# Tokens in runs of nine on a partition, and kv on 64x64 quarters

## The chip, the cores and the metric

The kernel runs on one core of one Trainium2 chip. The metric is device time in microseconds of a whole execution; the kernel before takes 289.03 us (median of 3 runs, 288.88 to 289.15). A profiled execution shows what each engine does: TensorE (PE, with its weight loads as PEld), VectorE (DVE), ScalarE (ACT), GpSimd (POOL) and the queues that issue transfers (SP, and ACT's own).

## What is computed

Attention in Shen's efficient form for 8 batches, 8 heads, 576 tokens and 64 dimensions: a softmax of q over the dimensions, a softmax of k over the tokens, a 64x64 matrix kv for each head, and x = q kv. Then a feed-forward block (FFN) with a gelu gate on the 4608 tokens of 512 features, with an inner width of 1536.

```python
q_s = np.exp(q - np.max(q, axis=-1, keepdims=True));  q_s /= np.sum(q_s, axis=-1, keepdims=True) + 1e-09
k_s = np.exp(k - np.max(k, axis=2, keepdims=True));   k_s /= np.sum(k_s, axis=2, keepdims=True) + 1e-09
kv = np.einsum('bhsd,bhse->bhde', k_s, v)
x  = np.einsum('bhsd,bhde->bhse', q_s, kv).transpose(0, 2, 1, 3).reshape(B * S, H * D)
g = x @ w_gate
out = 0.5 * g * (1.0 + erf(g / np.sqrt(2))) * (x @ w_val) @ w_out
```

Inputs and output are float32 in DRAM; the kernel multiplies in float16 and sums in float32.

## The kernel before

**Order.** The FFN runs over groups of 512 tokens: the first 512 tokens of each of eight batches, and one group (number 8, tile `xtr`) made of the 64 tokens that each batch leaves over. The groups come in the order 0 to 6, 8, 7. Groups 0 and 1 use plain products; from group 2 on, and partly in the output of group 1, products are by Strassen's scheme (7 products of half size, with sums of operands made on DVE, ACT and POOL). From group 2 on, the order of all work is written out in strings (`PROG`); in groups 0 and 1 attention for the next batch is hung into the FFN's loop by `plan`, filled with `at(...)` and played by `ride` (L1061 to L1108).

**Layout of q, k, v.** A batch's token number is m*9 + n, with m from 0 to 63. `load` (L180) puts each m on two partitions: an even one with token chunks n = 0 to 3 behind a padding, an odd one with n = 4 to 8. So there are five chunks of 128 partitions (`NC`), all eight heads lie on each partition, and one load is two transfers over 64 partitions, with runs of 1024 and 1280 bytes. The padding is written once by memsets (L151, L152, L158 and, for the second k buffer, on POOL): -1e30 for k, 0 for v and q. In batch 0, the odd half of each load goes by ACT's queue, the rest by SP's.

**Attention.** `exp` runs on ACT over the whole tile or half of the heads, padding included. For q, `norm_sum` and `norm_pair` (L241, L250) sum over the dimensions and take reciprocals on DVE, and `norm_mul` (L263) scales on POOL or DVE. `cast_v` copies v to float16, with a column of ones that gives the sum over k. kv is then made in one of three ways. Batch 0: `kv0_mm` (L340), ten 128x64 matmuls for each head pair, with k's sums from `ksum_mm` (L327). Batch 1: `kv_mm` (L304), five 128x128 matmuls with 130 columns for each head pair, of which a mask keeps the diagonal blocks. Batches 2 to 7: `unit_kv4` (L361), 40 matmuls with 128 partitions of k, 64 columns of weights and 65 columns of v into one PSUM bank, and `kv4_norm` (L374), one reciprocal and one product on DVE. q is transposed on TensorE in batches 0 and 1 (`unit_t`, L391) and by one transposing transfer in later ones (`unit_td`, L415).

x comes from `unit_x` (L438) in batches 0 and 1, one matmul with a block-diagonal 128x128 kv for each head pair, 512 columns. From batch 2 on `unit_x4` (L454) makes it with 64x64 quarters: eight narrow matmuls for the 64 remaining tokens (`psxr`) and eight of 512 columns (`psx`). A copy by ACT and DVE puts x into `xt`, in the order of tokens in which `store` (L585) writes the rows out again.

**The start.** L1001 to L1055: SP and ACT issue q, k, v; ACT loads its table for exp and writes the tile `warm`, on which TensorE runs 15 + 2 + 3 warm-up matmuls; weights follow on SP's queue, the first 256 columns of the gate's and the value's weights in two pieces by columns. `ffn_first0` (L551) then starts the FFN of batch 0 with the two upper head pairs' x still to be made between its matmuls, and `ffn_first` (L527) does the same in batch 1, whose list `first1` (L1077) has half of that batch's transposes, kv and x.

**Batch 0 to batch 1.** The output products of batch 0 (`psy`, L579) run in two sweeps over four blocks of 128 tokens; between them `plan` puts the first half of batch 1's attention, and `evac` (L988) takes the results out. POOL casts the last three pieces of the output weights. Sums of weights for Strassen's scheme (`sum_w`, `sum_wgv`) are spread over groups 0 and 1; the last two of `sum_wgv` (L642) run on DVE in the output of group 1.

Of the kernel before, what the change touches and what calls it, by code (L numbers as in the profile page):

```python
# [9 lines left out]
f32 = mybir.dt.float32  # L10
# [8 lines left out]
def kernel(  # L19
# [23 lines left out]
    NM = 4  # L43
    NC = NM + 1
    MAIN = NM * P
    REM = S - MAIN
    VW = D + 1
    WCH = [0, 128, 256] + list(range(512, F + 1, 256))
    NW = len(WCH) - 1
# [69 lines left out]
    mask = const.tile([P, 2, D], f32)  # L119
# [3 lines left out]
    for i in range(2):  # L123
        eq_b.append(const.tile([P, NC, C], f16, name=f"eq{i}"))
    ek_b.append(const.tile([P, NC, C], f16, name="ek"))
    v16_b.append(const.tile([P, NC, H, VW + 1], f16, name="v16"))
# [5 lines left out]
    eq0r = const.tile([P, C], f16)  # L132
    ld_b = {nm: [const.tile([P, H, NC * D], f32, name=f"{nm}t{i}") for i in range(n)]
# [5 lines left out]
    cc_b = [x.rearrange("p n c -> p (n c)").bitcast(f32)[:, 0:1024].rearrange(  # L139
# [5 lines left out]
    q0r = [x[0:64].rearrange("p (h d) -> p h d", d=D) for x in (  # L145
        kt1[:, 36 * P:].bitcast(f32), eq_b[1].rearrange("p n c -> p (n c)").bitcast(f32)[:, 1024:])]
# [4 lines left out]
    nc.vector.memset(ld_b["k"][0][:, :, 0:D], -1e30)  # L151
    nc.vector.memset(ld_b["v"][0][:, :, 0:D], 0.0)  # L152
    nc.vector.memset(tiny, 0.0)
    nc.vector.memset(ones, 1.0)
    nc.vector.memset(mask, 0.0)
    nc.vector.memset(mask[0:64, 0, :], 1.0)
    nc.vector.memset(mask[64:128, 1, :], 1.0)
    nc.vector.memset(ld_b["q"][0][:, :, 0:D], 0.0)  # L158
    make_identity(nc, ident)
    nc.gpsimd.memset(v16_b[0][:, :, :, D:D + 1], 1.0)  # L160
    nc.gpsimd.memset(ld_b["k"][1][:, :, 0:D], -1e30)
# [8 lines left out]
    QUAD = 2  # L170

    def heads(x, b, h0, h1):

        if b >= QUAD:
            return x.rearrange("p (t c) x -> p c t x", t=2)[:, h0 // 2:h1 // 2]
        return x[:, h0:h1]

    tiles = {}

    def load(src, nm, b, h0, h1, n0):  # L180
        tiles[(nm, b)] = buf(ld_b[nm], b)
        for t, c0 in ((0, n0), (1, 1)):
            (nc.scalar if b == 0 and t == 1 else nc.sync).dma_start(  # L183
                out=tiles[(nm, b)][t:P:2, h0:h1, c0 * D:NC * D],
                in_=src[b, h0:h1].rearrange("h (m n) d -> m h (n d)", n=NT)[
                    :, :, (4 * t + c0) * D:(4 * t + NC) * D])

# [6 lines left out]
    def load_w_gv(c):  # L194
        for w, nm in ((moe_w_gate, "wg"), (moe_w_val, "wv")):
            t = wst_tile(f"{nm}st", HP, WCH[c + 1] - WCH[c])
            nc.sync.dma_start(
                out=t, in_=w.rearrange("(ci p) f -> p ci f", p=P)[:, :, WCH[c]:WCH[c + 1]])
            wst[(nm, c)] = t
# [9 lines left out]
    def cast_w(nm, c, eng="pool"):  # L209
        dst = (wg_sb if nm == "wg" else wv_sb)[:, :, WCH[c]:WCH[c + 1]]  # L210
        copy_on(eng, dst, wst[(nm, c)])

    def load_w_o(c):
        t = wst_tile("wost", 2, C)
        nc.sync.dma_start(
            out=t, in_=moe_w_out.rearrange("(fi p) m -> p fi m", p=P)[:, 2 * c:2 * c + 2, :])
        wst[("wo", c)] = t

    def cast_w_o(c, eng="pool"):
        copy_on(eng, wo_sb[:, 2 * c:2 * c + 2, :], wst[("wo", c)])  # L220


    def exp(nm, b, h0=0, h1=H, n0=0):
        dst = ek_b[0] if nm == "k" else buf(eq_b, b)
        o, i = (("p n (c t d) -> p c t n d", "p c t (n d) -> p c t n d") if b >= QUAD else
                ("p n (h d) -> p h n d", "p h (n d) -> p h n d"))
        nc.scalar.activation(  # L227
            out=dst[:, n0:NC, h0 * D:h1 * D].rearrange(o, d=D, **({"t": 2} if b >= QUAD else {})),
            in_=heads(tiles[(nm, b)], b, h0, h1)[..., n0 * D:NC * D].rearrange(i, d=D),
            func=ACTF.Exp)  # L230

    def cast_v(b, h0, h1, eng="pool"):
        if h1 - h0 > 2 and (eng == "pool" or b >= QUAD):
            for h in range(h0, h1, 2):
                cast_v(b, h, h + 2, eng)
            return
        copy_on(eng, v16_b[0][:, :, h0:h1, 0:D].rearrange("p n h d -> p h n d"),
                (tiles[("v", b)][:, h0 // 2::4] if b >= QUAD else tiles[("v", b)][:, h0:h1]).rearrange(
                    "p h (n d) -> p h n d", d=D))

    def norm_sum(b, hp, n0=0):  # L241
        n = NC - n0
        e = buf(eq_b, b)[:, n0:NC, hp * P:(hp + 1) * P].rearrange("p n (h d) -> p n h d", d=D)
        rq = att.tile([P, n, 2], f32, name="rq", tag="rq", bufs=4)
        nc.vector.reduce_sum(rq, e, axis=mybir.AxisListType.X)
        rrq = att.tile([P, n, 2], f32, name="rrq", tag="rrq", bufs=4)
        nc.vector.reciprocal(out=rrq, in_=rq)
        st[(b, "norm", hp)] = (e, rrq, n)

    def norm_pair(b, g, n0, engs):  # L250

        n = NC - n0
        e = buf(eq_b, b)[:, n0:NC, 2 * g * P:(2 * g + 2) * P].rearrange("p n (h d) -> p n h d", d=D)
        rq = att.tile([P, n, 4], f32, name="rq2", tag="rq2", bufs=2)
        nc.vector.reduce_sum(rq, e, axis=mybir.AxisListType.X)  # L255
        rrq = att.tile([P, n, 4], f32, name="rrq2", tag="rrq2", bufs=2)
        nc.vector.reciprocal(out=rrq, in_=rq)
        for j in range(2):
            st[(b, "norm", 2 * g + j)] = (e[:, :, 2 * j:2 * j + 2], rrq[:, :, 2 * j:2 * j + 2], n)
        for j, eng in enumerate(engs):  # L260
            norm_mul(b, 2 * g + j, eng)

    def norm_mul(b, hp, eng="dve"):  # L263
        e, rrq, n = st[(b, "norm", hp)]
        (nc.gpsimd if eng == "pool" else nc.vector).tensor_tensor(  # L265
            out=e, in0=e, in1=rrq.unsqueeze(-1).to_broadcast((P, n, 2, D)), op=ALU.mult)

    def norm_mul2(b, hp, cut):
        e, rrq, n = st[(b, "norm", hp)]
        for eng, r in ((nc.vector, slice(0, cut)), (nc.gpsimd, slice(cut, n))):  # L270
            eng.tensor_tensor(out=e[:, r], in0=e[:, r], in1=rrq[:, r].unsqueeze(-1).to_broadcast(
                (P, r.stop - r.start, 2, D)), op=ALU.mult)

    def norm(b, hp, eng="dve", n0=0):
        norm_sum(b, hp, n0)
        norm_mul(b, hp, eng)

    def load_rem0():
        for h0 in (0, 4):
            nc.sync.dma_start(out=q0r[h0 // 4], in_=q[0, h0:h0 + 4].rearrange(  # L280
                "h (m n) d -> m h (n d)", n=NT)[:, :, 0:D])

    def exp_rem0():
        for i in range(2):
            nc.scalar.activation(
                out=eq0r[0:64, i * 4 * D:(i + 1) * 4 * D].rearrange("p (h d) -> p h d", d=D),
                in_=q0r[i], func=ACTF.Exp)

    def norm_rem0():
        e = eq0r[0:64].rearrange("p (h d) -> p h d", d=D)  # L290
        rq = att.tile([64, H], f32, name="rq0", tag="rq0", bufs=1)
        nc.vector.reduce_sum(rq, e, axis=mybir.AxisListType.X)
        rrq = att.tile([64, H], f32, name="rrq0", tag="rrq0", bufs=1)
        nc.vector.reciprocal(out=rrq, in_=rq)
        st["rrq0"] = rrq

    def norm_rem0_mul():
        e = eq0r[0:64].rearrange("p (h d) -> p h d", d=D)
        nc.gpsimd.tensor_tensor(
            out=e, in0=e, in1=st["rrq0"].unsqueeze(-1).to_broadcast((64, H, D)), op=ALU.mult)  # L300
# [3 lines left out]
    def kv_mm(b, g, j):  # L304
        if (b, "pskv", g) not in st:
            st[(b, "pskv", g)] = small([P, 2, 2 * VW], f32, "pskv")
        hp = 2 * g + j
        for n in range(NC):
            nc.tensor.matmul(
                st[(b, "pskv", g)][:, j, :], ek_b[0][:, n, hp * P:(hp + 1) * P],  # L310
                v16_b[0][:, n, 2 * hp:2 * hp + 2, 0:VW],
                start=(n == 0), stop=(n == NC - 1))

    def kv_norm(b, g):
        pskv = st[(b, "pskv", g)]
        rck = att.tile([P, 2], f32, name="rck", tag="rck")
        nc.vector.reciprocal(out=rck, in_=pskv[:, :, D])
        for j in range(2):
            kv_sb = att.tile([P, 2, D], f16, name="kv_sb", tag="kv", bufs=8)
            nc.vector.scalar_tensor_tensor(  # L320
                out=kv_sb,
                in0=pskv[:, j, :].rearrange("p (h e) -> p h e", e=VW)[:, :, 0:D],
                scalar=rck[:, j:j + 1], in1=mask, op0=ALU.mult, op1=ALU.mult)
            st[(b, "kv", 2 * g + j)] = kv_sb
# [849 lines left out]
```

## Time and profile before

| | |
|---|---|
| runs, median of 3 | 289.03 us (288.88 to 289.15) |
| span of the profiled execution | 286.9 us |
| outside of the span, median less span | 2.1 us |
| PE, DVE, ACT, POOL busy | 277.9, 248.3, 209.8, 137.9 us |
| DRAM read, written | 37.75 MB, 9.44 MB |

The span is the profiled execution's own time; what lies around it is start and end of the program. TensorE is the busiest engine. The profile's slices are 7.2 us each. Some stretches of it:

| stretch, us | what runs | PE busy | DVE busy | POOL busy | GB/s |
|---|---|---|---|---|---|
| 0 to 5 | loads, memsets, first warm-up matmul | 0.09 | 1.95 | 1.34 | 140 |
| 5 to 15 | attention of batch 0 | 9.90 | 7.07 | 4.36 | 363 to 389 |
| 15 to 18.6 | first FFN matmuls, rest of x of batch 0 | 3.60 | 1.84 | 2.37 | 389 |
| 18.6 to 36.9 | gate and value of batch 0 | 18.30 | 11.53 | 12.92 | 391 |
| 36.9 to 48.5 | output of batch 0, attention of batch 1 | 11.60 | 9.77 | 5.85 | 390 |
| 48.5 to 71 | gate and value of batch 1 | 22.50 | 17.64 | 20.36 | 325 |
| 71 to 82 | output of batch 1, kv and x of batch 2 | 10.85 | 10.80 | 3.36 | 77 |
| 82 to 287 | the rest | 201.07 | 187.69 | 87.34 | 127 |

A matmul's duration in the profile runs from its start to its modelled end, and neighbours overlap: what a step costs on TensorE is read from the start of its first matmul to the start of the next step's first.

### The profile page before, as it was taken

The numbers are of one execution on the slowest core, as the hardware profiler recorded it, in microseconds if no ns is written. First come the engines' busy times: TensorE is split into PE (matmuls) and PEld (weight loads), VectorE is DVE, ScalarE is ACT, GpSimd is POOL, SyncE is SP. The second block draws the span as 40 slices with busy tenths as digits, with TensorE's granted clock in tenths as the row PEclk, the third lists the DMA queues.
The fourth block names the chain that finished last, engine by engine and source line by source line (L and its number), as shares of the span: only waits on it lengthen the run. The fifth ranks groups of instructions, "written<-read, shape, count | busy, mean of one in ns | idle before, by whom it ended". The sixth has DMA issues, their size and how long they took to land.

```text
span 286.9 us, 6704 instructions
## 1 busy us (share of the span) xinstructions
PE 277.9 (97%) x2581; PEld 216.4 (75%) x2581; DVE 248.3 (87%) x497; ACT 209.8 (73%) x370; POOL 137.9 (48%) x128
## 2 busy tenths in 40 slices
PE   3999999999999999999999999999999999999994
PEld 1544445445888888888888888888888888888883
DVE  2854788877999999979989998999999799998993
ACT  3773367884798889978998899799794577716740
POOL 1557845987339721865864258542553104110110
PEclk9999999999999999999999999999999999999999
DMA  6999999999139916159149853690304030003303
GB/s 215 375 380 386 401 393 390 394 328 243 35 139 339 258 34 223 78 101 321 45 98 308 289 164 150 182 249 2 147 6 90 0 150 0 2 0 77 73 2 146
DMA packets 54623, 51.74 MB, mean 180 GB/s; under 512 B 18496, under 2 KB 50496, under 8 KB 54592
## 3 DMA queue, kind: packets, MB, share of 16 engines
q1 hardware_dynamic: 52864, 49.49, 54.0%
q10 hardware_dynamic: 1728, 1.84, 2.0%
q8 instruction: 20, 0.33, 0.5%
q14 instruction: 11, 0.09, 0.1%
HBM read 37.75 MB, written 9.44 MB: 164 GB/s over the span
## 4 chain that ended last, share of the span: by engine, by line
PE 91%; DVE 5%; ACT 1%; issue 1%; ACTq 1%; DVEq 0%
PE psa L670 24%; PE psc L670 12%; PE psA L749 12%; PE psg L511 7%; PE psv L511 7%; PE psC L749 6%; PE psb L670 6%; PE psy L579 4%; PE psB L749 3%; PE pswarm L503 2%; PE pskv L368 1%; PE psa L749 1%; DVE rq L255 1%; ACTq L183 1%; DVE yo L770 1%
## 5 line engine op out<-in xcount | busy, mean ns | idle before, releaser
L670 PEld LDWEIGHTS <-wgv_sb 128*128 128x128 f16 x672 | 65.7, 98 | 8.0 <-issue 0.3
L265 POOL TENSOR_TENSOR eq<-eq,rrq 128x640 f16<-128x640 f16 (+1 forms) x27 | 34.9, 1303 | 24.3 <-ACT psb L858 11.7
L749 PEld LDWEIGHTS <-ht 128*128 128x128 f16 x384 | 37.2, 98 | 5.3 <-issue 0.4
L670 PE MATMUL psa<-xs,wgv_sb 128*128 128x256 f16 x288 | 40.4, 273 | 0.1
L511 PEld LDWEIGHTS <-wgv_sb 128*128 128x128 f16 x192 | 18.6, 98 | 21.9 <-issue 0.2
L858 ACT COPY psb<-psa 128x512 f32<-128x512 f32 x42 | 24.2, 583 | 8.3 <-PE psa L670 8.1
L511 PE MATMUL psv<-xt,wgv_sb 128*128 128x512 f16 x96 | 26.6, 379 | 0.0
L511 PE MATMUL psg<-xt,wgv_sb 128*128 128x512 f16 x96 | 26.6, 379 | 0.0
L516 ACT ACTIVATE gl<-psg 128x512 f32<-128x512 f32 x24 | 13.8, 597 | 16.7 <-PE psg L511 16.7
L517 DVE SCALAR_TENSOR_TENSOR ht<-psv,gl 128x512 f16<-128x512 f32 x24 | 16.1, 686 | 10.5 <-PE psv L511 8.7
L839 ACT ACTIVATE snq<-psc 128x512 f32<-128x512 f32 x35 | 20.6, 602 | 5.7 <-PE psc L670 5.6
L227 ACT ACTIVATE ek<-kt 128x1280 f16<-128x1280 f32 (+1 forms) x11 | 19.2, 1758 | 5.9 <-DMA kt<-in_k_dram 4.2
L670 PE MATMUL psb<-xt,wgv_sb 128*128 128x256 f16 x144 | 21.6, 273 | 0.0
L670 PE MATMUL psa<-xt,wgv_sb 128*128 128x256 f16 x144 | 21.0, 273 | 0.0
L255 DVE TENSOR_REDUCE rq<-eq 128x20 f32<-128x1280 f16 (+1 forms) x12 | 17.1, 1424 | 4.4 <-ACT eq L227 4.4
L749 PEld LDWEIGHTS <-sh 128*128 128x128 f16 x192 | 18.6, 98 | 2.8 <-issue 0.4
L749 PE MATMUL psA<-tw,ht 128*128 128x256 f16 x168 | 20.6, 272 | 0.0
L227 ACT ACTIVATE eq<-qt 128x2560 f16<-128x2560 f32 (+2 forms) x10 | 18.4, 1861 | 2.6 <-DMA qt<-in_q_dram 2.6
L886 POOL TENSOR_TENSOR ht<-cc 128x512 f16<-128x512 f32 x12 | 15.3, 1274 | 9.1 <-ACT cc L884 8.8
L876 DVE SCALAR_TENSOR_TENSOR ht<-psb,gl 128x256 f16<-128x256 f32 x42 | 17.1, 412 | 1.8 <-ACT gl L874 1.6
L874 ACT ACTIVATE gl<-psa 128x256 f32<-128x256 f32 x42 | 16.1, 385 | 3.4 <-PE psa L670 2.9
L874 ACT ACTIVATE gl<-psb 128x256 f32<-128x256 f32 x42 | 15.5, 382 | 3.8 <-PE psb L670 3.4
(192 smaller groups left out, 694.8 us busy)
## 6 DMA issues: line engine op xcount, KB each, us to landing
out_dram<-yo SPq DMA_DIRECT2D x15, 512.0 KB, 3.5
kt<-in_k_dram SPq DMA_DIRECT2D x7, 640.0 KB, 8.3
vt<-in_v_dram SPq DMA_DIRECT2D x7, 640.0 KB, 7.2
qt<-in_q_dram SPq DMA_DIRECT2D x7, 640.0 KB, 7.0
qt<-in_q_dram SPq DMA_DIRECT2D x8, 512.0 KB, 7.5
wost<-in_moe_w_out_dram SPq DMA_DIRECT2D x6, 512.0 KB, 7.9
kt<-in_k_dram SPq DMA_DIRECT2D x6, 512.0 KB, 7.4
vt<-in_v_dram SPq DMA_DIRECT2D x6, 512.0 KB, 6.6
```

The lines of the kernel that those rows point to most:

```text
L227: nc.scalar.activation(out=dst[:, n0:NC, h0 * D:h1 * D].rearrange(o, d=D, **({"t": 2} if b >= QUAD else {})), in_=heads(tiles[(nm, b)], b, ...
L255: nc.vector.reduce_sum(rq, e, axis=mybir.AxisListType.X)
L265: (nc.gpsimd if eng == "pool" else nc.vector).tensor_tensor(out=e, in0=e, in1=rrq.unsqueeze(-1).to_broadcast((P, n, 2, D)), op=ALU.mult)
L511: nc.tensor.matmul(ps, w[:, ci, fi * P:(fi + 1) * P], xt[:, ci, :], start=(ci == 0), stop=(ci == HP - 1))
L517: nc.vector.scalar_tensor_tensor(out=ht[:, fi, :], in0=psv, scalar=_H_SCALE, in1=gl, op0=ALU.mult, op1=ALU.mult)
L670: nc.tensor.matmul(ps[:, t], a, x, start=(first and t == 0 and c == 0), stop=(c == 1), skip_group_check=True)
L749: nc.tensor.matmul(ps[t], a, w, start=(first and j == js[0] and (t == ts[0] or ps[t].tensor is not ps[ts[0]].tensor)), stop=(j == js[-1]), ...
L839: nc.scalar.activation(out=dst, in_=src, func=ACTF.Copy, scale=scale)
L858: nc.scalar.copy(out=t[f"b{k}"], in_=t[f"a{k}"])
L874: nc.scalar.activation(out=gl, in_=t[ps][:, 1], func=ACTF.Gelu)
L876: nc.vector.scalar_tensor_tensor(out=ht[:, k if x[2] == "2" else k + NO // 2, 0:256], in0=t[ps][:, 0], scalar=_H_SCALE, in1=t["g" + ps], o ...
L886: (nc.vector if side == "dve" else nc.gpsimd).tensor_tensor(out=ht[:, k:k + NO // 2 + 1:NO // 2, 256:512], in0=cc[:, :, 0], in1=cc[:, :, 1 ...
```

## The change

The tokens of a head stay together. A partition now holds one m of one half of the heads (64 partitions for heads 0, 2, 4, 6 and 64 for heads 1, 3, 5, 7, with four heads on each), and all nine chunks n of it: runs of 2304 bytes, one transfer over 128 partitions, and no padding.

```diff
-    def load(src, nm, b, h0, h1, n0):
+    def load(src, nm, b, a0=0, a1=HP, n0=0, eng=None):
         tiles[(nm, b)] = buf(ld_b[nm], b)
-        for t, c0 in ((0, n0), (1, 1)):
-            (nc.scalar if b == 0 and t == 1 else nc.sync).dma_start(
-                out=tiles[(nm, b)][t:P:2, h0:h1, c0 * D:NC * D],
-                in_=src[b, h0:h1].rearrange("h (m n) d -> m h (n d)", n=NT)[
-                    :, :, (4 * t + c0) * D:(4 * t + NC) * D])
+        base = src[b, 0]
+        (eng or nc.sync).dma_start(
+            out=tiles[(nm, b)][:, a0:a1, n0 * D:NT * D],
+            in_=bass.AP(tensor=base.tensor, offset=base.offset + 2 * a0 * S * D + n0 * D,
+                        ap=[[NT * D, P], [2 * S * D, a1 - a0], [1, (NT - n0) * D]]))
```

kv is made on quarters of the array, one for each of (half of the partitions, half of the columns), in two PSUM banks, with the scaling in two steps for each bank:

```diff
+    def quarters(j):
+        for hh in range(2):
+            for t in range(2):
+                yield 2 * j + t, hh, t, slice(64 * hh, 64 * hh + 64), slice(64 * t, 64 * t + 64)
...
     def unit_kv4(b, spare=False):
-        ps = st[(b, "pskv4")] = big([P, HP, VW], f32, "pskv", True) if spare else small([P, HP, VW], f32, "pskv")
-        for hp in range(HP):
-            for n in range(NC):
-                for s in range(2):
-                    c0 = hp * P + s * D
-                    nc.tensor.matmul(
-                        ps[s * D:(s + 1) * D, hp, :], ek_b[0][:, n, c0:c0 + D],
-                        v16_b[0][:, n, 2 * hp + s, 0:VW], start=(n == 0), stop=(n == NC - 1))
+        ps = st[(b, "pskv4")] = [big([P, 2, VW], f32, "pskv", True) if spare else
+                                 small([P, 2, VW], f32, "pskv") for _ in range(2)]
+        for j in range(2):
+            for n in range(NT):
+                for a, hh, t, r, o in quarters(j):
+                    nc.tensor.matmul(ps[hh][o, j, :], ek_b[0][r, n, a * D:(a + 1) * D],
+                                     v16_b[0][r, n, a, 0:VW], start=(n == 0), stop=(n == NT - 1))
```

x of batches 0 and 1 is made with eight quarters of 512 columns in place of four block-diagonal matmuls. Since the tokens of q's transpose now lie in another order, the copies of x permute them, so that rows are stored as before:

```diff
+    def xt_out(b, j, t, eng, ps):
+        copy_on(eng, get_xt(b)[:, 2 * j + t, :].rearrange("p (c m u) -> p c u m", c=(NT - 1) // 2, u=2),
+                ps.rearrange("p (u c m) -> p c u m", c=(NT - 1) // 2, u=2))
```

The transposing transfer becomes two, over 64 partitions each; that of batch 1's remaining tokens becomes two transposes on TensorE and a copy on ACT:

```diff
     def unit_td(b):
-        t = att.tile([P, NC * C], f16, name="eqt", tag="eqt").rearrange(
-            "p (n h t) -> p n h t", n=NC, h=HP)
-        nc.sync.dma_start_transpose(out=t.rearrange("p n h t -> p (n h) t"),
-                                    in_=buf(eq_b, b).rearrange("p n c -> p (n c)"))
+        t = att.tile([P, NT * C2], f16, name="eqt", tag="eqt")
+        for h in range(2):
+            nc.sync.dma_start_transpose(
+                out=t[:, h * NT * P:(h + 1) * NT * P].rearrange("p (n m) -> p n m", m=D),
+                in_=buf(eq_b, b)[64 * h:64 * h + 64].rearrange("p j n x -> p (j n x)"))
```

The start is put together anew. SP issues q in two pieces; k and v of batch 0 come in four pieces each, by turns on SP's and ACT's queue, ACT's after its table load. `warm` is set by DVE. Warm-up matmuls are 15 + 4 + 3 + 2 + 1. The first weight piece is cut by rows (1024-byte runs) instead of columns (512-byte runs).

```diff
+    for a in (0, 2):
+        load(q, "q", 0, a, a + 2, 1)
     preload(ACTF.Exp)
-    nc.scalar.copy(out=warm, in_=tiny[:, 1:2].to_broadcast((P, 512)))
+    for src, nm in ((k, "k"), (v, "v")):
+        for a in range(HP):
+            load(src, nm, 0, a, a + 1, 0, nc.scalar if a % 2 else nc.sync)
...
     warm_pe(15)
+    t_mm(0, 0)
+    warm_pe(4)
+    kv_banks(0)
+    ksum_mm(0, 0)
+    t_out(0, 0, "act")
+    ksum_rec(0, 0)
+    cast_vn(0, 0, (0, 3, 6, 9), ("dve", "act", "pool"))
+    warm_pe(3)
+    ksum_mm(0, 1)
+    ksum_rec(0, 1)
+    t_mm(0, 1)
+    kv_mm(0, 0)
+    t_out(0, 1, "dve")
+    kv_norm(0, 0, ("dve", "act"))
+    cast_vn(0, 1, (0, 3, 6, 9), ("dve", "act", "pool"))
+    warm_pe(2)
+    unit_x(0, 0, True)
+    kv_mm(0, 1)
+    warm_pe(1)
```

In `ffn_first` batch 0's second half of x stands behind the gate matmuls of the first two tiles; batch 1 has nothing left to do there. The rest of batch 0's gate and value matmuls go in pairs of tiles, two gates and then two values (`ffn_group`). The plan for groups 0 and 1 moves with it: all of batch 1's kv and x are made in the second sweep of batch 0's output, the last piece of the output weights is loaded and cast in halves behind v of batch 1, the casts of pieces 4 and 5a go from POOL to ACT, and the last two weight sums go from DVE to POOL:

```diff
+    at(0, NS, 3, L(t_mm, 1, 0), L(t_out, 1, 0, "dve"))
+    at(0, NS, 15, L(t_mm, 1, 1), L(t_out, 1, 1, "dve"), L(cast_v, 1, 0, "act"), L(cast_v, 1, 1, "pool"))
+    at(0, NS, 16, L(cast_v, 1, 2, "act"), L(cast_v, 1, 3, "pool"),
+       L(load_batch, 2, ((v, "v"),)))
+    at(0, NS, 17, L(kv_banks, 1), L(unit_kv, 1), L(cast_w_o, 5, "pool", 1, 2))
+    at(0, NS, 6, L(unit_x, 1, 0, True), L(unit_x, 1, 1, False, ()), L(sum_w, 3, "pool"))
+    at(0, NS, 8, L(x_out, 1, 1), L(sum_w, 1), L(sum_w, 2, "pool"), L(exp, "q", 2), L(preload, ACTF.Gelu))
...
-    at(1, NS, 2, L(sum_wgv, "g", 3), L(sum_wgv, "v", 3))
+    at(1, NS, 0, L(sum_wgv, "g", 3, 0, NO // 2, "pool"), L(sum_wgv, "v", 3, 0, NO // 2, "pool"))
```

The `PROG` strings are the same.

## The prediction

> **What bounds the kernel now.** I read the page first: busy times, slices, chain. Then the TensorE timeline at the places where the change adds or removes matmuls, the DVE, ACT and POOL timelines where their work moves, and the DMA issues with their landings.
>
> ```profile
> PE 277.9 (97%) x2581; PEld 216.4 (75%) x2581; DVE 248.3 (87%) x497; ACT 209.8 (73%) x370; POOL 137.9 (48%) x128
> ...
> PEclk9999999999999999999999999999999999999999
> DMA  6999999999139916159149853690304030003303
> ...
> PE 91%; DVE 5%; ACT 1%; issue 1%; ACTq 1%; DVEq 0%
> ```
>
> TensorE is busy for 277.9 of 286.9 us at full granted clock and makes up 91% of the chain. So a step costs what it adds to TensorE's own sequence, or the time for which TensorE waits. DMA is full until slice 10 (about 50 us at 7.2 us a slice): before that a landing can bound, later hardly.
>
> ```profile
> 12.78 0.38 PE L400 MATMUL pst<-ident,eq 128*128 128x128 f16 x4
> 13.13 0.74 PE L346 MATMUL pskv<-v,ek 128*64 128x64 f16 x20
> 13.92 0.39 PE L450 MATMUL psx<-eqt,kv_sb 128*128 128x256 f16 x2
> ...
> 14.96 0.39 PE L511 MATMUL psg<-xt,wgv_sb 128*128 128x512 f16 x1
> ...
> 16.29 0.38 PE L441 MATMUL psx<-eqt,kv_sb 128*128 128x512 f16 x1
> 16.60 0.35 PE L346 MATMUL pskv<-v,ek 128*64 128x64 f16 x10
> ...
> 18.57 0.38 PE L511 MATMUL psg<-xt,wgv_sb 128*128 128x512 f16 x1
> ```
>
> This is TensorE at the start (start, us, engine, line, output<-inputs, count). The first useful FFN matmul starts at 14.96, and attention still stands between the FFN's matmuls. The 96 gate and value matmuls of batch 0 end at 36.85; at 0.2156 us each (four in 0.86) they are 20.7 us, so they could have begun at 16.15: 1.2 us is lost after 14.96.
>
> ```profile
> 76.19 0.82 PE L368 MATMUL pskv<-v,ek 128*64 128x65 f16 x40
> 76.95 0.83 PE L749 MATMUL psc<-wo_sb,s 128*128 128x256 f16 x6
> ...
> 80.64 1.47 PE L749 MATMUL psa<-tw,ht 128*128 128x256 f16 x12 [0.15 <-DVE yo L770]
> ...
> 106.48 0.26 PE L462 MATMUL psxr<-eqt,kv 64*64 64x64 f16 x8
> 106.56 0.60 PE L462 MATMUL psx<-eqt,kv 64*64 64x512 f16 x8
> 107.10 0.50 PE L749 MATMUL psC<-wo_sb,s 128*128 128x256 f16 x3
> ```
>
> The step that builds kv takes from 76.19 to 76.95: 0.75 us for 40 matmuls, 18.8 ns each. The step that builds x, already on 64x64 quarters, takes 106.48 to 107.10.
>
> **Edit 1: kv on quarters, batches 2 to 7.** 40 matmuls become 72 of 64x64 with 65 columns. The table of before has 64x64 quarters with 64 columns only inside the x step. With 8 of them beside the eight wide ones that step takes 0.62 us; where 8 more ride along (224.53 to 225.27) it takes 0.74. So 8 more cost 0.12 us: 15 ns each, 72 cost 1.08, and a batch pays 0.33 more. Lower end: starts in that group lie some 10.5 ns apart, so 72 cost 0.76 and the batch pays nothing. Upper end: 0.62 less two rounds of 0.2156 leaves 0.19 for 8, so 24 ns each, 1.73 in all, 0.98 more. In between, the 18.8 ns of L368 gives 1.35, or 0.6 more. I take 15 ns, since that row has shape, column count and order of quarters. Six batches: +2.0 us, all on TensorE's path (between 0 and +5.9; 3.6 at 18.8 ns). The scaling of kv becomes two reciprocals and two products of 128 elements (0.92 against 0.60 on DVE, from rows of 0.17 and of 0.42 for 256), but two reductions over 1152 instead of 1280 return 0.27: nothing, hidden by TensorE's other matmuls.
>
> The Trainium skill ("TensorE: Matmul & The Clock Gate", Part 1) states that matmul starts never come closer than about 25 ns however narrow, which speaks against many small ones; its Part 3 has tiles in different row groups start about 4 ns apart. By the first 72 would be 1.8 us and the six batches 6.3 us slower; the 18.8 ns row here already lies below 25, so I give it no weight.
>
> **Edit 2: the start.** Out go the padding's memsets, the mask, and 10% of exp's elements of k; loads become one DMA over 128 partitions with 2304-byte runs, k and v by head pair from two queues. Warm matmuls may begin about 3 us sooner (before, 4.9 us were waited for ACT's L1004), off the path. Walked with rows of before: q halves land by 5.2 and 7.0 where turns are by whole transfers (packets of 2.2 to 4.0 us are all ACT's), then 381 to 395 GB/s; exp of 1024 takes 1.05 and of 1152 1.15 (0.836 ns each plus 0.19), so exp of k ends at about 11.55; eqt copy and v cast end at 13.1, kv of the first half at 13.5, its scaling 13.85, x 14.3, the copies 14.45 to 15.1. The first FFN matmul is at 15.05 to 15.1, 0.1 later. But then only 0.25 us of x and about 0.3 of waiting for gelu (after its table load) come between, against 1.2: the gate and value matmuls end near 36.35, a gain of 0.5. Bounds: if the whole of q comes first and k follows with no sharing, first matmul 14.0, gain 1.6; if the two queues share from 4.3 on, 15.7, gain 0; if the first SP transfer is slow as the isolated one (first packets 1.4 us after issue), a loss of 0.6.
>
> The Trainium skill ("DMA: Bandwidth & Descriptors", Queues, rings and completion order) has each DMA engine take turns between queues packet by packet. Here q10's packets were alone from 2.2 to 4.0; by the page the start would gain 0.
>
> **Edit 3: batch 0 to batch 1.** Before, half of batch 1's attention lay inside its FFN (48.5 to 52); now all of it must be done before the first FFN matmul. Work on TensorE: eight quarters of 0.216 in two or three rounds (0.45 to 0.54) against four of 0.216, 72 quarters at 15 ns (1.08) against 20 at 128x130 (1.14), two transposes more (0.11): 0.3 less. New wait: behind the last kv matmul only three matmuls of 0.216 (0.65) cover the reciprocal and two scalings on each engine (0.17 + 2 x 0.35 = 0.87): 0.22 open. Then one matmul (0.22) covers x's copy (0.59 on ACT) and what is left before it of yo's evacuation (0.60, of which I put 0.26 still to run): 0.63 open. Together 0.85; less the 0.3, I take +0.5. What is late next is gelu of batch 1's first tile, and its product on DVE. Lower end 0. Upper end +1.2: v of batch 1 landed at 47.2 before (POOL's cast waited 1.53 us for it) and all four heads are now needed. One transfer of 256 KB (0.65 us at 390 GB/s) is moved behind it, so it lands at about 46.5, its casts (0.68) end at 47.2, and TensorE reaches kv at about 47.0. A larger gain at the start would mostly be spent waiting there.
>
> **Edit 4: 71 to 82 us.** DVE is busy 10.80 of these 11 us. The two weight sums (L642, 1.56 for both) leave it for POOL, idle from 70.4 to 76.6. The wait at 80.64 and some 0.2 us before it go: −0.3 (0 to −0.4). If POOL is late, the sums delay the first matmuls of batch 2, which read them after 82.
>
> **Edit 5: DMA transposes.** One of 128 by 2560 becomes two of 64 by 2304. Landing was 4.9 to 8.9 us after issue; two behind each other on SP I put at 9.2 at worst (5.9 of issuing plus the tail), and the shortest distance from issue to use is 10.7 (213.83 to 224.5). SP's later loads and stores queue 1 to 3 us longer; the stores' 3.5 us of landing have room. Zero; 1 to 2 us if one is late. The permuted writes of x (4-byte stride) I put at the plain copies' 0.59 and 0.68 us; DVE's cover is TensorE's strip of psC and psA matmuls, and twice the price would cost about 0.5 us a batch.
>
> **Sum.** −0.5 + 0.5 − 0.3 + 2.0 = +1.7 on a span of 286.9, so 288.6. The median of the runs is 289.03, 2.1 above the span; I leave that as it is: 290.7.
>
> **Rivals.**
> A, faster: the start and the loads. Longer runs bring everything sooner: at 410 GB/s (best slices late in the trace) instead of 390 the 17.5 us up to v of batch 1 shrink by 0.85, so the full 1.6 passes that place. With 12 ns a quarter (0.86, +0.11 each, +0.7) the sum is −1.6 + 0.5 − 0.3 + 0.7 = −0.7, 288.3. It decides (faster by over 0.58) from the point where a quarter costs less than 12.3 ns. For: 512-byte runs moved at 347 GB/s, 1280-byte ones at 381 to 395. Against: that these are near the best already.
> B, no change: quarters at 11 ns (0.79, +0.04 each, +0.3) against −0.3 of the rest: 289.0. For: the starts 10.5 ns apart. Against: the 0.12 us for eight.
> C, clearly slower: quarters cost what L368's do, 18.8 ns: −0.3 + 3.6, 292.3. For: each needs its own weight load as L368's do. Against: again the 0.12 us.
> D, the layout doesn't give what it says: SP's transposes late, +1.5 on top: 292.2. Little speaks for it beside the longer queue.
>
> **Numbers.** The forecast (289.8 to 291.6) gets 0.42, A 0.25, B 0.15, C 0.13, D 0.05. A measurement of this kernel tells no change from within 0.2% (0.58 us). So faster 0.26, within 0.17 (B, and edges of A and the forecast), slower 0.57. The range takes in A and reaches to C: 287.9 to 292.3.
>
> **What would show it.** The new kv step should take 1.08 us in batches 2 to 7, with the x step still 0.62; 0.8 would make A or B right, 1.35 C. Batch 0's gate and value matmuls should end at about 36.35, the first FFN matmul at 15.1. A wait of TensorE of some 0.85 us should stand just before batch 1's first FFN matmul. Near 80.6 no wait for DVE. Wrong would be: waits of TensorE in batches 3 to 7 before the x step (transposes) or after it (copies of x), neither of which the sum holds.

## The result, and the profile after

| | before | after |
|---|---|---|
| median | 288.95 us (4 runs, 288.82 to 289.15) | 291.58 us (4 runs: 290.79, 290.90, 292.27, 292.39) |
| ratio after to before | | 1.0092, 95% interval 1.0067 to 1.0117 |
| span of the profiled execution | 286.9 | 288.9 (its run took 290.90) |
| PE, DVE, ACT, POOL busy | 277.9, 248.3, 209.8, 137.9 | 279.0, 244.6, 209.5, 137.3 |

The change costs 2.6 us by the medians, and the profiled execution shows 2.0 of it. The four runs fall into two pairs 1.45 us apart; the lower pair has granted clocks (the mean clock that TensorE was given, as a share of full speed) of 1.0 and 0.997 over the span, the upper pair 0.994. Why is a matter of its own, taken up with the experiments.

First the page of the changed kernel (busy times; slices) and TensorE's table of waits (engine, line, what it waited for: us in total, times, longest).

```profile
PE 279.0 (97%) x2923; PEld 215.7 (75%) x2923; DVE 244.6 (85%) x491; ACT 209.5 (73%) x379; POOL 137.3 (48%) x130
...
PE   8799999999699999999999999999999999999994
```

```profile
PE psc L673 <- DVE sh L550: 1.8, 1, 1.8
PE pst L345 <- POOL eq L239: 1.6, 1, 1.6
...
PE psa L673 <- DVE gl L690: 0.4, 1, 0.4
PE psg L446 <- DVE xt L193: 0.4, 1, 0.4
```

The one 6 among the 9s is slice 11, 72 to 79 us, and the largest wait after the start is for a DVE sum, `sh`, that the change does not touch. The second one lies in the start, between warm-up matmuls and the first transposes.

To place the difference, the same points of TensorE's sequence are read in both timelines (start of the first matmul named):

| point, us | before | after | later by | gained or lost since the row above |
|---|---|---|---|---|
| output of batch 0 (`psy`) | 36.69 | 36.12 | −0.57 | −0.57 |
| output of batch 1 (`psa`) | 70.68 | 70.26 | −0.42 | +0.15 |
| x of batch 2 (`psxr`) | 79.67 | 81.69 | +2.02 | **+2.44** |
| x of batch 3 | 106.48 | 108.56 | +2.08 | +0.06 |
| x of batch 7 | 224.53 | 226.68 | +2.15 | +0.07 |
| end of the span | 286.9 | 288.9 | +2.0 | −0.1 |

Everything that is lost is lost in nine microseconds, in the output of batch 1. TensorE, then DVE, then POOL in that stretch of the changed kernel (in brackets: the engine's idle time just before, and what ended it):

```profile
72.88 1.04 PE L673 MATMUL psc<-tw,sh 128*128 128x256 f16 x8
75.73 0.61 PE L673 MATMUL psc<-tw,sh 128*128 128x256 f16 x4 [1.81 <-DVE sh L550]
76.79 1.48 PE L673 MATMUL psa<-tw,sh 128*128 128x256 f16 x12 [0.45 <-DVE gl L690]
78.20 0.83 PE L321 MATMUL pskv<-v,ek 64*64 64x65 f16 x72
78.97 1.48 PE L673 MATMUL psc<-wo_sb,s 128*128 128x256 f16 x12
```

```profile
71.76 0.68 DVE L452 SCALAR_TENSOR_TENSOR ht<-psv,gl 128x512 f16<-128x512 f32 x1
72.36 1.53 DVE L550 TENSOR_TENSOR s<-ht,sh 128x1024 f16<-128x1024 f16 x1
73.82 1.85 DVE L550 TENSOR_TENSOR sh<-ht 128x512 f16<-128x512 f16 x1
75.70 0.42 DVE L550 TENSOR_TENSOR sh<-sh,ht 128x512 f16<-128x512 f16 x1
```

```profile
71.26 4.13 POOL L566 TENSOR_TENSOR wgv_sb<-wgv_sb 128x768 f16<-128x768 f16 x2
```

From 71.26 to 75.4 POOL makes the two weight sums that the change gave it. In just that time two of DVE's float16 sums take 1.53 and 1.85 us. The same sums took 0.67 and 0.41 before, when POOL was idle up to 76.61; DVE, then POOL, of the kernel before:

```profile
72.65 0.67 DVE L626 TENSOR_TENSOR s<-ht,sh 128x1024 f16<-128x1024 f16 x1
73.25 0.41 DVE L626 TENSOR_TENSOR sh<-ht 128x512 f16<-128x512 f16 x1
```

```profile
76.61 3.36 POOL L203 CAST v<-vt 128x640 f16<-128x640 f32 x4 [6.23 <-PE pskv L368]
```

The product that reads PSUM, at 71.76, takes 0.68 in both. TensorE's third product waits for the slow sum. The kv step, 78.20 to 78.97, takes 0.77 us for its 72 quarters.

### The profile page after: what moved, and what is told of

Same layout as the page of the kernel before. It is cut to its first block, busy times and chain, and to the rows that moved or that the text cites. A ratio compares the mean times of both kernels' runs of the same rounds, so it can differ in the third digit from the quotient of the medians.

```text
span 288.9 us, 7376 instructions
## 1 busy us (share of the span) xinstructions
PE 279.0 (97%) x2923; PEld 215.7 (75%) x2923; DVE 244.6 (85%) x491; ACT 209.5 (73%) x379; POOL 137.3 (48%) x130
## 3 DMA queue, kind: packets, MB, share of 16 engines
q10 hardware_dynamic: 720, 1.44, 1.3%
## 4 chain that ended last, share of the span: by engine, by line
PE 67%; DVE 4%; ACT 1%; issue 1%; DVEq 0%
PE psa L594 25%; PE psc L594 12%; PE psA L673 11%; PE psb L594 6%; PE psC L673 6%; PE psB L673 3%; PE pskv L321 1%; PE psa L673 1%; DVE sh L550 1%; PE psx L386 1%; DVE ht L800 1%; PE psc L673 0%; DVE cc L766 0%; DVE xt L193 0%; ACT L441 0%
## 5 line engine op out<-in xcount | busy, mean ns | idle before, releaser
L239 POOL TENSOR_TENSOR eq<-eq,rrq 128x576 f16<-128x576 f16 (+1 forms) x28 | 34.5, 1244 | 25.1 <-ACT psb L782 10.8
L231 DVE TENSOR_REDUCE rq<-eq 128x18 f32<-128x1152 f16 (+1 forms) x16 | 21.2, 1324 | 5.2 <-ACT eq L213 5.0
L446 PE MATMUL psg<-xt,wgv_sb 128*128 128x512 f16 x96 | 23.8, 379 | 0.5 <-DVE xt L193 0.4
L446 PE MATMUL psv<-xt,wgv_sb 128*128 128x512 f16 x96 | 23.8, 379 | 0.0
L213 ACT ACTIVATE ek<-kt 128x1152 f16<-128x1152 f32 (+1 forms) x11 | 17.7, 1605 | 5.6 <-issue 4.4
L213 ACT ACTIVATE eq<-qt 128x1152 f16<-128x1152 f32 (+1 forms) x16 | 17.6, 1149 | 3.7 <-DMA qt<-in_q_dram 3.7
L550 POOL TENSOR_TENSOR sh<-ht 128x512 f16<-128x512 f16 x7 | 8.1, 1157 | 20.2 <-PE psc L594 11.1
L800 DVE SCALAR_TENSOR_TENSOR ht<-psa,gl 128x256 f16<-128x256 f32 x42 | 17.2, 417 | 0.2 <-ACT gl L798 0.2
```

Source lines behind the costliest of these rows:

```text
L213: nc.scalar.activation(out=o.rearrange("p n (a d) -> p a n d", d=D), in_=tiles[(nm, b)][:, 2 * i0:2 * i1, n0 * D:NT * D].rearrange("p a (n ...
L239: (nc.gpsimd if eng == "pool" else nc.vector).tensor_tensor(out=e, in0=e, in1=rrq.unsqueeze(-1).to_broadcast((P, n, D)), op=ALU.mult)
L446: nc.tensor.matmul(ps, w[:, ci, fi * P:(fi + 1) * P], xt[:, ci, :], start=(ci == 0), stop=(ci == HP - 1))
L550: (nc.gpsimd if eng == "pool" else nc.vector).tensor_tensor(out=o, in0=a, in1=b, op=op)
L800: nc.vector.scalar_tensor_tensor(out=ht[:, k if x[2] == "2" else k + NO // 2, 0:256], in0=t[ps][:, 0], scalar=_H_SCALE, in1=t["g" + ps], o ...
```

## The experiments

**1. The weight sums, on either kernel.** The theory after the comparison: POOL's two sums hold up DVE's float16 sums, and that is the whole loss. Rival: the new layout leaves DVE with too much work there.

```diff
-    at(1, NS, 0, L(sum_wgv, "g", 3, 0, NO // 2, "pool"), L(sum_wgv, "v", 3, 0, NO // 2, "pool"))
+    at(1, NS, 2, L(sum_wgv, "g", 3), L(sum_wgv, "v", 3))
```

> The changed kernel with one edit undone: the last two weight sums (g3, v3) back on DVE behind the second product of group 1's output, as before the change. Contention theory (POOL's 4.13 us of sums at 71.3 to 75.4 slow the float16 sums that DVE runs beside them, 0.67 to 1.53 us and 0.41 to 1.85 us, and TensorE waits 1.8 us for the result): DVE's sums take 0.67 and 0.41 again, the wait before the third product goes, and the span falls by 2.2 to 2.6 us from 288.9, to 286.3 to 286.7, time about 288.4 to 288.8. Rival (DVE is late there because the new layout gives it more work in that stretch): DVE gets 1.6 us more to do, the wait stays or grows, span 288.9 or more.

Measured: 288.92 us (11 runs, 288.78 to 289.46), ratio to before 1.0005 (0.9996 to 1.0013). The wait for `sh` is gone and the sums take 0.68 and 0.41 us:

```profile
72.48 0.68 DVE L550 TENSOR_TENSOR s<-ht,sh 128x1024 f16<-128x1024 f16 x1
73.08 0.41 DVE L550 TENSOR_TENSOR sh<-ht 128x512 f16<-128x512 f16 x1
```

The median is 2.66 us under the changed kernel's, the profiled span 1.7 under: less than the 2.2 to 2.6 expected, since DVE with 1.9 us more to do now makes TensorE wait 0.81 us at 81.07 for `yo`. So the prediction's reason for the edit, DVE's load, was a real one; what it left out cost more.

The same edit the other way round, on the kernel before:

```diff
-    at(1, NS, 2, L(sum_wgv, "g", 3), L(sum_wgv, "v", 3))
+    at(1, NS, 0, L(sum_wgv, "g", 3, 0, NO // 2, "pool"), L(sum_wgv, "v", 3, 0, NO // 2, "pool"))
```

> The kernel before with only that one edit made: the two sums on POOL, right behind the first product of group 1's output. Contention theory: DVE's 1024-wide sums beside them go from 0.67 to about 1.5 us, TensorE waits about 2 us before the third product, span 286.9 + 2 to 2.6, time 291 to 291.7. The prediction's edit 4: 0.3 us faster, 288.7. Rival (only the new layout suffers): no change, 289.0.

Measured: 290.73 us (4 runs, 290.66 to 290.79), ratio 1.0065 (1.005 to 1.0081): 1.9 us lost by two lines in the old layout, a little less than the 2 to 2.6 expected. Its DVE and POOL timelines show the mechanism once more:

```profile
71.68 1.52 DVE L626 TENSOR_TENSOR ht<-ht 128x1024 f16<-128x1024 f16 x1
73.13 0.68 DVE L517 SCALAR_TENSOR_TENSOR ht<-psv,gl 128x512 f16<-128x512 f32 x1
73.73 1.53 DVE L626 TENSOR_TENSOR s<-ht,sh 128x1024 f16<-128x1024 f16 x1
75.18 0.41 DVE L626 TENSOR_TENSOR sh<-ht 128x512 f16<-128x512 f16 x1
```

```profile
70.57 4.14 POOL L642 TENSOR_TENSOR wgv_sb<-wgv_sb 128x768 f16<-128x768 f16 x2
```

POOL ends at 74.7; the sum that starts after that takes its old 0.41. The layout rival falls: its loss does not need the layout.

**2. The sums on POOL, but later.**

```diff
-    at(1, NS, 0, L(sum_wgv, "g", 3, 0, NO // 2, "pool"), L(sum_wgv, "v", 3, 0, NO // 2, "pool"))
+    at(1, NS, 2, L(sum_wgv, "g", 3, 0, NO // 2, "pool"), L(sum_wgv, "v", 3, 0, NO // 2, "pool"))
```

> The changed kernel with the two sums kept on POOL but later, behind kv of batch 2, where DVE reads PSUM for most of its work. If POOL slows only DVE's float16 SBUF-to-SBUF sums, the sums of 71 to 76 us are quick again and the PSUM readers (0.68 us) stay at 0.68: span 286.3 to 287, with v's casts on POOL 3 to 4 us later and perhaps a wait in batch 2's first products of up to 1 us. If POOL slows everything on DVE, the wait only moves by some microseconds: span 288 to 289.

Measured: 288.49 us median of 10 runs; eight lie at 288.32 to 288.59 (spans 286.3 to 286.6, as expected), two at 289.98 and 290.37. POOL runs v's casts first and the sums at 80.71 (3.24 us), beside copies of x out of PSUM, which keep their time (two in 1.34 us, 1.32 with POOL idle). So it is the float16 sums out of SBUF that suffer, not DVE as a whole; the one such pair in that stretch, `xs`, takes 1.05 instead of 0.73.

The profiled execution is one of the two, with a clock of 0.994. Its stretches 5 to 9, 9 to 13 and 13 to 17 us (stretch, width, PE busy and matmuls, granted clock, DMA share, GB/s):

```profile
5.00:9.00 4.00, 1.97 (x7) 1.00 1.04 407
9.00:13.00 4.00, 3.87 (x51) 0.57 1.00 356
13.00:17.00 4.00, 3.92 (x128) 1.00 1.09 382
```

TensorE idles 2.15 us before the first transposes (9.13), the granted clock is then at half for 3.4 us (below: half rate), and the first FFN matmul comes at 16.43 instead of 14.66 us. The gap is the change's: warm-up matmuls begin at 1.36 us instead of 4.91 and are over at 6 to 7.3, while the transposes still wait until 8.9 for POOL's scaling of q.

**3. Is it that gap?** First a closed gap in the changed kernel.

```diff
-    warm_pe(15)
+    warm_pe(25)
     t_mm(0, 0)
-    warm_pe(4)
+    warm_pe(2)
```

> The changed kernel with 25 warm-up matmuls ahead of q's first transposes instead of 15, and 2 instead of 4 behind them; the weight sums stay on POOL where the change puts them. Gap theory (TensorE is idle for 1.6 to 2.9 us between the last warm-up matmul and the transposes, and in some runs the granted clock falls to half for 3.4 us behind that gap, which costs about 1.5 us): the gap shrinks to 1.2 us or less, every run has a clock of 0.997 or more, and all lie at 290.7 to 291.1 instead of one half at 290.8 and the other at 292.3. Rival (the slower runs have a cause elsewhere, say the wait at 74 to 77 us): runs at 292.3 with a clock of 0.994 remain in a similar share.

A miss: 292.3 us, four runs of 292.24 to 292.37, three with clocks of 0.992 to 0.994 and one, unexplained, with 1.0. In the profiled one the gap at the start is closed and the clock there is 1.0, but a half-rate stretch stands elsewhere: 3.4 us from about 77.4 on, 1.7 us after TensorE has resumed (75.64) behind a wait of 1.82 us for DVE's sums, and behind a second one of 0.45 (columns as above):

```profile
74.00:75.00 1.00, 0.00 (x0) 1.00 0.00 0
75.00:76.00 1.00, 0.35 (x4) 1.00 0.00 0
76.00:77.00 1.00, 0.55 (x6) 1.00 0.00 0
77.00:78.00 1.00, 1.00 (x9) 0.69 0.00 0
78.00:80.00 2.00, 2.00 (x77) 0.50 0.03 8
```

So the change opens two gaps of about 2 us, and half rate was seen behind either. Which of the two it was in the changed kernel's own upper pair is not known, as only a run of the lower pair was profiled. That the gap causes it is not shown by this run. Then fewer warm-up matmuls ahead of the transposes, to lengthen the gap, with the sums late:

```diff
-    warm_pe(15)
+    warm_pe(11)
     t_mm(0, 0)
-    warm_pe(4)
+    warm_pe(8)
```

> The late sums on POOL, with 11 warm-up matmuls ahead of the transposes instead of 15 (and 8 instead of 4 behind them): the gap is made longer by 0.9 to 1.7 us. Gap theory: most runs now have a granted clock of about 0.994 and take 1.5 us longer, 290 to 290.4. Rival: the same mixture as the late sums alone, mostly 288.5.

Measured: 290.87 us, four runs of four at 290.8 to 291.1 with clocks of 0.993 and 0.994: +2.4 against 288.49 (part of that is eight warm-up matmuls running at half rate on the path, first FFN matmul 17.02). The profiled one:

```profile
8.85 0.62 PE L345 MATMUL pst<-ident,eq 128*128 128x128 f16 x8 [2.61 <-POOL eq L239]
9.30 3.23 PE L438 MATMUL pswarm<-warm,ident 128*128 128x512 f16 x8
```

And the closed gap with the sums late, in two forms, 25 + 2 and 25 + 0 warm-up matmuls:

> The late sums on POOL together with the 25 + 2 warm-up matmuls: the version in which both found losses are mended. Expected 288.3 to 288.6 in every run, none at 290, faster than before by 0.3 to 0.5 us. If the extra warm-up matmuls delay the transposes in the critical chain of the start, up to 0.5 us slower than the late sums alone (288.49).

Measured: 288.90 us (12 runs, 288.45 to 290.29), ratio 1.0003 (0.9991 to 1.0014): no clock under 0.997, but a wide spread, and in the profiled execution the transposes came at 9.71 and the first FFN matmul at 15.04, pushed back by the warm-up matmuls. Two runs at 290.09 and 290.29 had no half-rate stretch on record; what they lost is not settled.

```diff
-    warm_pe(15)
+    warm_pe(25)
     t_mm(0, 0)
-    warm_pe(4)
     kv_banks(0)
```

> The late sums on POOL with 25 warm-up matmuls ahead of q's first transposes and none between them and the sums of k (25 + 0 + 3 + 2 + 1): the gap is closed as with 25 + 2, and the first sums of k are no longer pushed back by the two behind the transposes. Expected: first FFN matmul at 14.6 to 14.8 us (25 + 2 had 15.04), every run at 288.2 to 288.6, none with a clock of 0.994: faster than before by 0.3 to 0.7 us. If gaps at the start are not the only source of the slower runs, some at 290 remain.

Measured: 288.59 us (11 runs, 288.41 to 289.61), ratio 0.9998 (0.9988 to 1.0008), all clocks 0.997 or more, first FFN matmul 14.59. Runs at 290 and above are gone here, but not in the version of experiment 5, which has the same warm-up; some at 289.0 to 289.6 remain. In the profiled one (span 287.1) TensorE waited 0.7 us for casts of the first weights.

So the warm-up ahead of the transposes governs the half-rate stretch at the start. Counted by clocks under 0.995: none of 34 runs with the gap closed (this experiment's 23 with the sums late, and the 11 of experiment 5), four of four with 11 warm-up matmuls, and with the change's own 15 two of ten here, none of eleven in experiment 1 and the one run of experiment 4 (idle 2.13 us; its profile has the clock at 0.5 from about 8.9 to 12.3). Three of 22 against none of 34 would not settle it; the four of four carry the finding. The length of the gap is not the whole of it: experiment 1's profiled execution idled 2.93 us there without a drop.

**4. What a quarter costs when there are more of them.** The kv step twice over, in all six batches and then in one.

```diff
-        for j in range(2):
+        for j in (0, 1, 0, 1):
             for n in range(NT):
                 for a, hh, t, r, o in quarters(j):
```

> The sums on DVE again as in the first of these runs, and the 72 quarter matmuls of kv run twice over in batches 2 to 7 (the second pass writes the same result). If a quarter costs what the trace of the changed kernel shows (72 in 0.77 us, 10.7 ns each) the span grows by 6 x 0.77 = 4.6 us over that first run; at the prediction's 15 ns it would grow by 6.5, at 18.8 ns by 8.1.

Measured: 305.41 us (one run), +16.5 instead of +4.6, with a mean clock of 0.981. The first step's 144 quarters go through in 1.37 us, 9.5 ns each; then TensorE waits 1.0 us for nothing but its own issue. Four such waits make 7.9 us, and the clock stands for some 5.8 more (an estimate, 0.019 of a span of 303.5), part of which lies in the start. TensorE's waits on issue:

```profile
PE pskv L321 <- issue: 5.7, 2, 3.8
...
PE psB L673 <- issue: 1.2, 1, 1.2
PE psc L673 <- issue: 1.0, 1, 1.0
```

> As the version with both mended, with the 72 quarter matmuls of kv run twice over in batch 4 alone (the second pass writes the same result). In the run that doubled them in all six batches, 16 us were added, with waits of TensorE on issue and with a lower granted clock. If one doubled step costs its array time alone, the stretch from batch 3's x step to batch 4's grows by 0.77 us and the time by the same. If the stream of 288 short instructions cannot be fed, a wait on issue of 1 us or more stands behind that step and the time grows by 2 to 3 us.

(there `for j in ((0, 1, 0, 1) if b == 4 else (0, 1)):`)

Measured: 295.61 us (one run, clock 0.988), some 7 us over the version it was built on. TensorE's timeline, and the DMA of one microsecond within the wait:

```profile
130.60 1.32 PE L321 MATMUL pskv<-v,ek 64*64 64x65 f16 x137
135.70 0.33 PE L321 MATMUL pskv<-v,ek 64*64 64x65 f16 x7 [3.77 <-issue]
135.95 2.74 PE L673 MATMUL psB<-wo_sb,ht 128*128 128x256 f16 x12
```

```profile
DMA packets 187, 0.41 MB, mean 408 GB/s; under 512 B 16, under 2 KB 16, under 8 KB 186
...
q8 instruction: 1, 0.02, 5.8%
```

After 137 quarters there is no instruction left for 3.77 us, while loads for the next batch move 408 GB/s; one packet of the instruction queue passes within that wait, at 133 to 134 us, and another after it. Where DMA stood idle (77 to 82 us in the kernel with all steps doubled) the wait was 1.0 us. 6.8 us at half rate followed. That the fetch is held up by the loads is the reading that fits; it was not tried with the loads moved away. The step with 72 quarters shows no such wait in any batch.

**5. The start on one queue.** To test the prediction's early bound:

```diff
-            load(src, nm, 0, a, a + 1, 0, nc.scalar if a % 2 else nc.sync)
+            load(src, nm, 0, a, a + 1, 0, nc.sync)
```

> As the one with 25 + 0 warm-up matmuls, but k and v of batch 0 all on SP's queue behind q, none on ACT's. The prediction's early bound (whole q first, then k with no sharing: first FFN matmul 14.0): q's second half lands about 1.2 us sooner (5.7 instead of 6.95), k's halves end their exp up to 1 us sooner, and the gate and value matmuls of batch 0 end 0.5 to 0.8 us sooner, time 287.6 to 288.2. The other way: SP's issues wait for room in its queue (in the changed kernel two of v's issues took 2.7 us together), v and the first weights land later, and the start is slower by 0.5 to 1.5 us, 288.8 to 290.

Measured: 288.65 us (11 runs, 288.25 to 290.8), ratio 0.9996 (0.9981 to 1.001): not to be told from the two-queue start (288.59). Yet what was expected of the transfers came:

```profile
4.23 1.06 ACT L213 ACTIVATE eq<-qt 128x1024 f16<-128x1024 f32 x1 [2.00 <-DMA qt<-in_q_dram]
5.50 1.06 ACT L213 ACTIVATE eq<-qt 128x1024 f16<-128x1024 f32 x1 [0.22 <-DMA qt<-in_q_dram]
7.89 1.16 ACT L213 ACTIVATE ek<-kt 128x1152 f16<-128x1152 f32 x1 [1.33 <-DMA kt<-in_k_dram]
9.46 1.16 ACT L213 ACTIVATE ek<-kt 128x1152 f16<-128x1152 f32 x1 [0.41 <-DMA kt<-in_k_dram]
```

q's second half is there at 5.5 instead of 7.0 and k's exp ends 0.5 us sooner, but the first FFN matmul starts at 14.61. TensorE came to the transposes only at 9.71 (8.92 in the two-queue profile), since the 25 warm-up matmuls took 8.51 us here (7.72 there), though POOL had ended its scaling of q at 8.46; from there to 14.61 its one marked wait is 0.15 us for the second v cast. So in this execution the warm-up matmuls, and not the transfers, set when the attention work began, with that cast as the next limit. Whether fewer of them would let the gain through was not tried. The one run of 290.8 has a clock of 1.0; what it lost is not known.

No version was found that beats the kernel before beyond doubt: the late sums (median 288.49 against 288.85, ratio 0.9999 with 0.9984 to 1.0014), and the two last, lie 0.1% under it by median, inside their intervals.

## Why the prediction was right in sign and wrong in its reasons

It gave 290.7 in 287.9 to 292.3 and slower as the likelier side; 291.58 was measured. That the sum came out near is luck: its largest term (+2.0) was nothing, and a term that it had as a gain (−0.3) was the loss (+2.44). About 0.7 of the 2.6 us between the medians comes from the two runs with a clock of 0.994, for which the sum had no term.

- **Edit 1, quarters at 15 ns, +2.0 us: the step that failed first.** 72 quarters took 0.71 to 0.77 us, 9.9 to 10.7 ns each, against 0.75 for the 40 before: 0. The lower end, the 10.5 ns between starts in the x step, was right. The 15 ns came from the one x step of 0.74 us minus the others' 0.62. In the changed kernel the same two kinds of step take 0.68 (226.68 to 227.36) and 0.65 us (108.56 to 109.21): 4 ns for each of the eight. So most of the 0.12 was not theirs, and one difference of two steps, divided by eight, was a poor price where the starts themselves are on the timeline. The statement of the Trainium skill that matmul starts never come closer than some 25 ns ("TensorE: Matmul & The Clock Gate", Part 1) is contradicted here by 9.5 to 10.7 ns between quarters in different row and column groups; the 4 ns of its Part 3 is not reached either.
- **Edit 2, the start, −0.5: right.** −0.57 in the profiled execution; first FFN matmul 14.66 instead of 15.1. What it left out was the price of "warm matmuls may begin about 3 us sooner, off the path": they ended sooner too, and the gap behind them puts a half-rate stretch into some runs.
- **Edit 3, batch 0 to batch 1, +0.5: +0.15.** The wait before batch 1's first FFN matmul came (0.75 us from 48.68 to 49.43 where 0.22 of matmul stands), on the copies of x as said. The work was over-priced: kv of batch 1 took 0.77, not 1.08.
- **Edit 4, 71 to 82 us, −0.3: +2.44, the step that decided.** It counted POOL's idle time and DVE's relief, and not what POOL's work does to DVE beside it. The trace of before had the answer, in lines it did not set side by side. DVE, then POOL, of the kernel before:

```profile
69.40 1.53 DVE L626 TENSOR_TENSOR sh<-sh,ht 128x1024 f16<-128x1024 f16 x1
```

```profile
68.78 1.60 POOL L651 TENSOR_TENSOR wgv_sb<-wgv_sb 128x512 f16<-128x512 f16 x1
```

One line, one shape: 1.53 us while POOL works, 0.67 while it does not (72.65, shown above). So a cost of moving 4.1 us of POOL work beside 2.2 us of such sums could have been foreseen. It is no fixed price for each sum, though: the 1024-wide one lost 0.86 us and the 512-wide one 1.44. In these rows a sum ends shortly after the POOL instruction that it met: POOL's ends at 70.38 and DVE's at 70.93 above; in the changed kernel POOL's two, 2.08 us each, end at 73.34 and 75.39 and DVE's at 73.89 and 75.67. What it loses is about what is left of that instruction. The Trainium skill says as much ("Trainium Architecture — The Big Picture", What this means for kernel authors): of the engines only DVE and GpSimd contend for a port, and as an exclusive lock. The traces agree for sums of float16 in SBUF, by the ends just given, and show none of it for the DVE instructions here that read PSUM (0.68 us beside POOL and without).
- **Edit 5, transposes and permuted copies, 0: right.** No wait for a transpose anywhere in TensorE's table; landings 4.1 to 7.1 us. The copies of x have medians of 0.74 us on ACT and 0.72 on DVE instead of the 0.59 and 0.68 that it put, which TensorE's other work hides: there is no wait behind them over 0.2 us later on.

Of the rivals, A and B had the quarters' price right (under 12.3 ns) and the sign wrong; C and D did not occur. With edit 4 undone (experiment 1) the kernel measured 288.92, which is B's 289.0. The reading that DMA is full until "about 50 us" was a slip (ten slices of 7.2 us are 72), on which no term of the sum rests. That a move which relieves the busiest helper engine could slow it was not among them.

## What to carry to other kernels

Before work is moved to POOL, look for the same DVE line in the trace once beside POOL work and once without: if it stretches, the move is paid by DVE, here with up to 1.44 us for one sum, and its place matters more than POOL's idle time (moved two steps later, the same sums cost nothing that shows in the time). Close a gap on TensorE by the time at which the next real work can start, not by the time at which warm-up can: a gap of 2 us that looks free was here followed by half rate in some runs. Price a short matmul by the starts of its own kind on the timeline, and give a large term that rests on a single difference of two rows its full bounds.

## What the hardware showed that was not expected

- A half-rate stretch of 3.4 us can follow an idle time of TensorE of 1.8 to 2.6 us, at 77 us as well as at the start. Runs with it took 1.4 to 1.9 us longer (2.4 with 11 warm-up matmuls), and it comes in some runs of one kernel and not in others: four of four with 11 warm-up matmuls (idle 2.61 us in the profiled one), three of 22 with 15 and without the wait at 74 us. One profiled execution with 2.93 us idle had none, so the length alone does not decide. Four runs (292.28, 290.29, 290.09 and 290.8 us) were about as slow with clocks of 0.997 to 1.0; why is open.
- Quarters of the array take 9.5 to 10.7 ns each, but only for as long as their instructions are there: 137 went through, then TensorE had 3.77 us of waiting for issue beside loads at 408 GB/s.
- POOL's own sums stretch as well beside DVE's: two take 4.13 us at 71 us and 3.24 where DVE mostly reads PSUM. The stretched DVE sums end 0.55 us (1024 wide) or 0.28 us (512 wide) after a POOL sum does.
